# Bank order of projection bursts and scores, and a longer lag of the softmax normalization, in a layernorm + attention + gated FFN kernel

## The chip, the cores and the metric

The kernel runs on one core of a Trainium2 chip. The metric is the device time of one execution in microseconds. A core has a matmul engine (TensorE, PE in the profile; PEld is its weight load), three engines for elementwise work (VectorE = DVE, ScalarE = ACT, GpSimd = POOL) and a queue engine (SyncE = SP). The program gives each engine one list of instructions. TensorE's results go to PSUM, here used as eight banks of 512 fp32 columns over 128 partitions; in this kernel DVE and ACT read them from there, and POOL works on SBUF alone.

## The reference

```python
x = A_x                                   # (1, 2048, 448) bf16
xn = _layernorm(x)
# A: attention of 16 query heads on 8 key/value heads (Dh 256), last W = 512 keys of the cache, no mask
q = (xn @ wq) per head
p = softmax(q @ k.T * 256 ** -0.5)
s = concat(p @ v) @ wo
# B: gated FFN, F = 1792
g = silu((gelu(xn @ w_gate) * (xn @ w_up)) @ w_down)
return x + s * g
```

## The kernel before, in words

**Order of work.** The kernel records operations by hand with a small recorder: every call of `pe`, `act`, `dve`, `pool`, `dma` or `dmaT` appends one operation to one engine's list and derives its waits from the tiles and banks that it reads and writes. The order in the code is therefore the order on each engine, and what waits there holds up what was recorded behind it.

**Stages.** The 2048 rows are four chunks of 512 (four tiles of 128 rows each). First comes the FFN for all chunks (to about 133 us); the last chunk's `down` is spread as filler into the first attention heads. Then attention runs over `NI` = 64 pairs of chunk and head (`i` = 16 * chunk + head) with four tiles each, so `n = 4 * i + t` counts 256 tiles.

**One tile of attention.** `scores(i, t)` issues two matmuls into one PSUM bank, chosen by `s_bank(n)`; DVE takes the row maximum (L563, `nmax`), ACT the exponential with the row sum (L565, `pr` and `den`; the sum comes out with a second small instruction). `normalize` takes the reciprocal of the sum on DVE (L570) and scales `pr` (L575 on DVE; for the first 28 tiles L572 on POOL), and then issues a transposing DMA on SP's queue (L253) from `pr` to `pT`. `LAG` says how many tiles `normalize` stands behind `scores` in the recorded order: one. There are 11 `pr` buffers.

**What follows a tile.** At even `t`, `values` (four matmuls into bank 0, 6 or 1, by a fixed pattern of eight) multiplies the transposed probabilities of a head some three heads back with V; its result is copied to `oT`, by ACT (L599), in the first heads partly by DVE (L597). At odd `t`, from head 7 on, half an output projection `outproj` (L620) of a group of four heads is issued, mostly into bank 7, and DVE adds it to `acc` (L641, L643). In chunks after the first, head 6 of the chunk has no output projection and head 2 has two (the second one in place of values). The last head of each chunk is "folded": V times wo is made once, and its `pT` (`pTf`) goes straight into the output projection.

**Bursts.** The queries of the next eight heads are projected in one go: `q_burst` is called at tile `t = 0` of heads 7, 15, 23, ... 55, right behind that tile's scores and values (and a burst of four heads at i = 3). A burst has `heads` parts; part `n` fills a pair of banks, the matmuls (L473) coming in two phases, with phase 0 of part n+1 ahead of phase 1 of part n:

```python
for n in range(heads + 1):
    if n < heads:
        part(n, 0)
    if n:
        part(n - 1, 1)
```

Phase 0 has 8 half-height matmuls (two run side by side), phase 1 has 6. After phase 1 ACT copies both banks to `qT` (L528). Pair 0 is banks 0 and 1, pair 1 is 2 and 3, pair 2 is 4 and 5; banks 6 and 7 take no part. The banks of scores (2 to 5) and of values (0, 1) are thus used by bursts as well. I call the work between two bursts a stretch: 32 tiles.

**The end.** After the last scores (n = 255) one `normalize` is left, then two letters per step say what comes: "v" is a `values` of heads 61 and 62, "o" one of the three output projections left of the group of heads 56 to 59. Then come the output projections of the last group, the final DVE steps (L631, L633) and the output DMAs.

Of the kernel before, what the change touches and what calls it, by code (L numbers as in the profile page):

```python
# [144 lines left out]
def bass_recurrent_scan__sliding_block_cached__geglu_ffn__prompt_kernel(nc, A_x, A_k, A_v, A_wq, A_wo, B_x, B_wg, B_wu, B_wd, out):  # L145
# [6 lines left out]
    QC, TPC, HP, KF = 512, 4, 64, 3  # L152
# [9 lines left out]
    with es:  # L162
# [89 lines left out]
        def dmaT(dst, src, w=(), r=(), after=(), lane=None):  # L252
            return R.op("sync", lambda e: e.dma_start_transpose(dst, src), r=r, w=w, dma=True, after=after, lane=lane)  # L253
# [211 lines left out]
        def two_blocks(ph, c, s, w, w6, keys, q0=0, q1=QC):  # L465


            def run(e):
                for k in range(KF + 1 - ph):
                    for lo in (0, HP):  # L470
                        m = (lo > 0) ^ ph
                        lhsT = w[m][lo:lo + HP, k, :] if k < KF else w6[lo:lo + HP, :]
                        ins = e.matmul(bank(s + m)[:, q0:q1], lhsT=lhsT, rhs=xnT[lo:lo + HP, c, k, q0:q1],  # L473
                                       start=ph == 0 and k == 0, stop=ph == 1 and k == KF - 1)
                return ins
            hard = [phase0[s]] if ph else []
            phase0[s] = pe(run, r=xn(c)[q0 // P:q1 // P] + keys, w=[("ps", s), ("ps", s + 1)], hard=hard)
# [16 lines left out]
        def down(c, t, part=range(NF)):  # L494
            b = (6, 7, 3, 7)[t] if c == NQC - 1 else 6 + t % 2
            for f in part:
                pe(lambda e, f=f: e.matmul(bank(b, D), lhsT=actT[:, f, t * P:(t + 1) * P], rhs=wd[:, f, :],  # L497
                                           start=f == 0, stop=f == NF - 1),
                   r=[("actT", f), ("wd",)], w=[("ps", b)])
            if NF - 1 in part and c < NQC - 1:  # L500
                act(lambda e: e.activation(gy[:, c * TPC + t, :], bank(b, D), ACT.Copy),
                    r=[("ps", b)], w=[("gy", c * TPC + t)])
            elif NF - 1 in part:
                dve(lambda e: e.tensor_copy(gy[:, c * TPC + t, :], bank(b, D)),
                    r=[("ps", b)], w=[("gy", c * TPC + t)])


        NI = NQC * Hq
        NG = NI // 4

        def q_slot(i):

            p = i // 2
            p = p if p < 3 else (p - 3) % NQP
            return qT[p], "qT%d" % p, i % 2

        def q_burst(i0, heads):

            c, h0 = divmod(i0, Hq)

            def part(n, ph):
                hp, e_ = divmod(n, 2)
                s, h = 2 * ((2, 0, 1, 2, 0, 2, 1, 0)[n] if heads == 8 else (0, 1, 2, 0)[n] if i0 else (n + 2) % 4), h0 + 2 * hp
                buf, name, _ = q_slot(i0 + 2 * hp)
                two_blocks(ph, c, s, [wq[:, :, h + m, e_ * P:(e_ + 1) * P] for m in range(2)],
                           wq6[:, h // 2, e_ * P:(e_ + 1) * P], wq_keys)
                if ph:
                    act(lambda e: e.activation(  # L528
                        buf[:, :, e_, :], psum[:, s * 512:(s + 2) * 512].rearrange("p (a q) -> p a q", a=2), ACT.Copy, scale=scale),
                        r=[("ps", s), ("ps", s + 1)], w=[(name, e_)])  # L530
# [6 lines that stand above are left out]
# [4 lines left out]
        def p_slot(i):  # L541

            n = (i - i // Hq) % NPT
            return (pTf, ("pT", "f")) if folded(i) else (pT[:, n, :, :], ("pT", n))


        LAG, FIRST = 1, 7 * TPC

        def s_bank(n):
            return (4, 5, 2)[n % 3] if n <= 3 * TPC else 2 + (n + 1) % 4  # L550

        def scores(i, t):
            g, n = (i % Hq) // 2, i * TPC + t
            b, s = s_bank(n), n % NPR
            buf, name, a = q_slot(i)

            def run(e):
                for k in range(NE):
                    ins = e.matmul(bank(b), lhsT=buf[:, a, k, t * P:(t + 1) * P], rhs=kT[:, g, k, :],  # L559
                                   start=k == 0, stop=k == NE - 1)  # L560
                return ins
            pe(run, r=[("kT", g), (name, 0), (name, 1)], w=[("ps", b)])
            dve(lambda e: e.tensor_reduce(nmax[:, s:s + 1], bank(b), mybir.AxisListType.X, ALU.max, negate=True),  # L563
                r=[("ps", b)], w=[("nmax", s)])
            act(lambda e: e.activation(pr[s][:, :], bank(b), ACT.Exp, bias=nmax[:, s:s + 1], accum_out=den[:, s:s + 1]),  # L565
                r=[("ps", b), ("nmax", s)], w=[("pr%d" % s,), ("den", s)])

        def normalize(i, t):
            s = (i * TPC + t) % NPR
            dve(lambda e: e.reciprocal(rden[:, s:s + 1], den[:, s:s + 1]), r=[("den", s)], w=[("rden", s)])  # L570
            if i * TPC + t < FIRST:
                pool(lambda e: e.tensor_tensor(pr[s][:, :], pr[s][:, :], rden[:, s:s + 1].to_broadcast([P, W]), ALU.mult),  # L572
                     r=[("pr%d" % s,), ("rden", s)], w=[("pr%d" % s,)])
            else:
                dve(lambda e: e.tensor_scalar(pr[s][:, :], pr[s][:, :], rden[:, s:s + 1], None, op0=ALU.mult),  # L575
                    r=[("pr%d" % s,), ("rden", s)], w=[("pr%d" % s,)])
            dst, key = p_slot(i)
            dmaT(dst[:, :, t * P:(t + 1) * P], pr[s][:, :], r=[("pr%d" % s,)], w=[(*key, t)], lane="p%d" % s)
# [22 lines left out]
        def n_pieces(G):  # L601
            return 3 * NE + NJ if folded(4 * G + 3) else 4 * NE
# [55 lines left out]
        def silu(n):  # L658

            s = n % 2  # L660
            act(lambda e: e.activation(tmp[:, s, :], gy[:, n, :], ACT.Tanh, scale=0.5), r=[("gy", n)], w=[("tmp", s)])  # L661
            pool(lambda e: e.tensor_scalar(tmp[:, s, :], tmp[:, s, :], 1.0, 0.5, op0=ALU.add, op1=ALU.mult),  # L662
                 r=[("tmp", s)], w=[("tmp", s)])
            pool(lambda e: e.tensor_tensor(gy[:, n, :], tmp[:, s, :], gy[:, n, :], ALU.mult),
                 r=[("tmp", s), ("gy", n)], w=[("gy", n)])
# [35 lines left out]
        for i in range(NI):  # L701
            for t in range(TPC):
                n = i * TPC + t
                scores(i, t)
                if n >= LAG:
                    normalize(*divmod(n - LAG, TPC))
                if 4 * i + t in fill:
                    down(NQC - 1, *fill[4 * i + t])

                early = i >= Hq and i % Hq == 2  # L710
                if t % 2 == 0 and early:
                    n = n_pieces(outs[1][0])
                    outproj(*outs[1], range(n * t // 4, n * (t + 2) // 4), b=6)
                elif t % 2 == 0 and 4 * i + t >= 12:
                    values(*pv.pop(0))
                if 7 <= i and t % 2 and not (i >= Hq and i % Hq == 6):
                    n = n_pieces(outs[0][0])
                    outproj(*outs[0], range(n * (t - 1) // 4, n * (t + 1) // 4))
                    if t == TPC - 1:
                        del outs[0:1 + early]  # L720
                if t == 0 and (i == 3 or i % 8 == 7) and i + 1 < NI:
                    q_burst(i + 1, 4 if i == 3 else 8)
            if i % Hq in (7, 9, 11, 13):
                silu(i // Hq * TPC + (i % Hq - 7) // 2)
        for n in range(NI * TPC - LAG, NI * TPC):
            normalize(*divmod(n, TPC))

        for what in "vvovovo":
            if what == "v":
                values(*pv.pop(0))  # L730
            else:
                outproj(*outs[0], range(n_pieces(outs.pop(0)[0])))
# [35 lines left out]
```

## Time and profile before

| | us |
|---|---|
| median of 3 runs | 572.48 (572.27 to 572.71) |
| profiled execution, its own time | 572.64 |
| span of the profiled execution | 570.8 |
| PE busy | 556.0 (97%) |
| DVE busy | 369.5 (65%) |
| ACT busy | 369.6 (65%) |
| POOL busy | 117.1 (21%) |
| PE in the chain that ended last | 82% |
| granted clock of TensorE | 1.000 |

Times in the trace are counted from the start of the span. A row of the timeline gives start, duration, engine, line, operation, tile written and read, and in brackets the idle time of the engine just before it and what ended that. A row of the chain gives start, duration and what the end of the program was waiting for in that time. A row of waits gives who waited for whom: total us, times, longest. An SPq row covers the issuing of DMAs by SP. A busy share is an average over the span; a matmul's duration is modelled and overlaps the next one's.

### The profile page before, as it was taken

How to read it: one execution, taken by the hardware profiler on the slowest of the kernel's cores; microseconds unless marked ns; L12 is line 12 of the kernel's file. 1: busy time of each engine (PE TensorE's matmuls, PEld its weight loads, DVE VectorE, ACT ScalarE, POOL GpSimd, SP SyncE). 2: the span in 40 equal slices, each digit the busy share in tenths (PEclk: the TensorE clock that was granted, in tenths of full speed). 3: DMA queues.
4: the chain of work that ended last, by engine and by line, in shares of the span. 5: the costliest groups of instructions: out<-in, count | busy, mean ns of one | idle time of the engine just before them, and what ended most of it. 6: DMA issues, size and time to landing. Idle time of an engine off the chain costs nothing.

```text
span 570.8 us, 10398 instructions
## 1 busy us (share of the span) xinstructions
PE 556.0 (97%) x3550; PEld 261.9 (46%) x3550; DVE 369.5 (65%) x939; ACT 369.6 (65%) x800; POOL 117.1 (21%) x153
## 2 busy tenths in 40 slices
PE   9999999999999999999999999999999999999997
PEld 6444444444443444344444444444444344444445
DVE  5626345145481998199639936992898199739984
ACT  5433334247676687676778867776888676768860
POOL 0131223104481121003301110140121003301133
DMA  8882546922443455155625632545456155635552
GB/s 227 290 152 57 138 77 116 275 65 69 78 92 56 76 101 93 29 101 95 140 54 93 103 74 50 98 96 120 66 101 100 31 101 91 144 50 93 97 101 53
DMA packets 165445, 57.69 MB, mean 101 GB/s; under 512 B 155649, under 2 KB 162305, under 8 KB 165393
## 3 DMA queue, kind: packets, MB, share of 16 engines
q1 hardware_dynamic: 162048, 44.64, 41.5%
q0 software_dynamic: 3040, 12.16, 8.1%
q8 instruction: 29, 0.48, 0.4%
q10 hardware_dynamic: 304, 0.22, 0.2%
q14 instruction: 24, 0.19, 0.1%
HBM read 17.92 MB, written 1.84 MB: 35 GB/s over the span
## 4 chain that ended last, share of the span: by engine, by line
PE 82%; DVE 13%; ACT 2%; issue 1%; DMA 1%; POOL 0%; ACTq 0%
PE ps L473 32%; PE ps L559 15%; PE ps L590 15%; PE ps L620 12%; PE ps L497 7%; DVE nmax L563 7%; DVE pr L575 3%; ACT qT L528 1%; DVE acc L641 1%; DVE acc L643 1%; DVE rden L570 1%; PE ps L348 1%; ACT oT L599 1%; DMA pT<-pr 1%; DVE oT L597 0%
## 5 line engine op out<-in xcount | busy, mean ns | idle before, releaser
L563 DVE TENSOR_REDUCE nmax<-ps 128x1 f32<-128x512 f32 x256 | 175.0, 684 | 111.1 <-PE ps L559 107.7
L565 ACT ACTIVATE pr<-ps,nmax 128x512 bf16<-128x512 f32 x256 | 175.9, 687 | 69.7 <-PE ps L590 35.4
L559 PE MATMUL ps<-kT,qT 128*128 128x512 bf16 x512 | 150.9, 379 | 0.5 <-ACT qT L528 0.5
L590 PE MATMUL ps<-pT,V 128*128 128x512 bf16 x480 | 123.1, 379 | 2.1 <-ACT oT L599 1.4
L620 PE MATMUL ps<-wo,oT 128*128 128x448 bf16 (+1 forms) x498 | 111.0, 346 | 0.4 <-DVE acc L641 0.4
L473 PE MATMUL ps<-xnT,wq 64*128 64x512 bf16 x896 | 99.5, 376 | 7.9 <-ACT qT L528 7.8
L575 DVE TENSOR_SCALAR pr<-pr,rden 128x512 bf16<-128x512 bf16 x228 | 86.7, 380 | 8.1
L528 ACT ACTIVATE qT<-ps 128x1024 bf16<-128x1024 f32 x64 | 64.5, 1023 | 36.0 <-PE ps L473 35.3
L473 PE MATMUL ps<-xnT,wu 64*128 64x512 bf16 x336 | 82.3, 376 | 0.0
L473 PE MATMUL ps<-xnT,wg 64*128 64x512 bf16 x336 | 82.0, 376 | 0.0
L491 DVE TENSOR_TENSOR actT<-ps,hb 128x512 bf16<-128x512 f32 x56 | 38.5, 692 | 65.9 <-ACT hb L490 61.7
L559 PEld LDWEIGHTS ps<-kT,qT 128*128 128x128 bf16 x512 | 49.4, 98 | 55.8 <-issue 3.4
L590 PEld LDWEIGHTS ps<-pT,V 128*128 128x128 bf16 x480 | 46.3, 98 | 60.7 <-ACT oT L599 5.6
L473 PEld LDWEIGHTS ps<-xnT,wq 64*128 64x128 bf16 x896 | 44.0, 94 | 62.8 <-ACT qT L528 11.3
L620 PEld LDWEIGHTS ps<-wo,oT 128*128 128x128 bf16 x498 | 48.4, 98 | 49.5 <-DVE acc L641 1.9
L599 ACT ACTIVATE oT<-ps 128x512 bf16<-128x512 f32 x113 | 66.4, 588 | 4.6 <-PE ps L590 4.5
L490 ACT ACTIVATE hb<-ps 128x512 bf16<-128x512 f32 x56 | 33.1, 594 | 38.5 <-PE ps L473 38.4
L565 ACT ACTIVATION_READ_ACCUMULATOR pr<-ps,nmax 128x1 f32 x256 | 50.4, 197 | 0.0
L647 POOL TENSOR_TENSOR tmp<-acc,gy 128x448 f32<-128x448 f32 x16 | 16.6, 1035 | 149.3 <-DVE acc L643 141.2
L497 PE MATMUL ps<-wd,actT 128*128 128x448 bf16 x224 | 46.5, 353 | 0.0
L662 POOL TENSOR_SCALAR tmp<-tmp 128x448 f32<-128x448 f32 x16 | 9.1, 566 | 164.3 <-ACT tmp L661 164.3
L473 PEld LDWEIGHTS ps<-xnT,wg 64*128 64x128 bf16 x336 | 31.3, 94 | 20.5 <-issue 1.1
(62 smaller groups left out, 350.8 us busy)
## 6 DMA issues: line engine op xcount, KB each, us to landing
pT<-pr SPq DMA_TRANSPOSE x240, 2.5
wq<-in_A_wq_dram POOLq DMA_DIRECT2D x14, 256.0 KB, 3.6
wo<-in_A_wo_dram POOLq DMA_DIRECT2D x3, 896.0 KB, 8.1
V<-in_A_v_cache_dram POOLq DMA_DIRECT2D x4, 448.0 KB, 6.5
xr<-in_A_x_dram POOLq DMA_DIRECT2D x4, 448.0 KB, 4.6
wd<-in_B_w_down_dram SPq DMA_DIRECT2D x1, 1568.0 KB, 14.2
x<-in_A_x_dram SPq DMA_DIRECT2D x3, 448.0 KB, 8.3
out_dram<-xr POOLq DMA_DIRECT2D x3, 448.0 KB, 3.8
```

The lines of the kernel that those rows point to most:

```text
L473: ins = e.matmul(bank(s + m)[:, q0:q1], lhsT=lhsT, rhs=xnT[lo:lo + HP, c, k, q0:q1], start=ph == 0 and k == 0, stop=ph == 1 and k == KF - 1)
L490: act(lambda e: e.activation(hb[:, h, :], bank(s), ACT.Gelu_apprx_tanh), r=[("ps", s)], w=[("hb", h)])
L491: dve(lambda e: e.tensor_tensor(actT[:, f, :], bank(s + 1), hb[:, h, :], ALU.mult), r=[("ps", s + 1), ("hb", h)], w=[("actT", f)])
L497: pe(lambda e, f=f: e.matmul(bank(b, D), lhsT=actT[:, f, t * P:(t + 1) * P], rhs=wd[:, f, :], start=f == 0, stop=f == NF - 1), r=[("actT", ...
L528: act(lambda e: e.activation(buf[:, :, e_, :], psum[:, s * 512:(s + 2) * 512].rearrange("p (a q) -> p a q", a=2), ACT.Copy, scale=scale), ...
L559: ins = e.matmul(bank(b), lhsT=buf[:, a, k, t * P:(t + 1) * P], rhs=kT[:, g, k, :], start=k == 0, stop=k == NE - 1)
L563: dve(lambda e: e.tensor_reduce(nmax[:, s:s + 1], bank(b), mybir.AxisListType.X, ALU.max, negate=True), r=[("ps", b)], w=[("nmax", s)])
L565: act(lambda e: e.activation(pr[s][:, :], bank(b), ACT.Exp, bias=nmax[:, s:s + 1], accum_out=den[:, s:s + 1]), r=[("ps", b), ("nmax", s)], ...
L575: dve(lambda e: e.tensor_scalar(pr[s][:, :], pr[s][:, :], rden[:, s:s + 1], None, op0=ALU.mult), r=[("pr%d" % s,), ("rden", s)], w=[("pr%d ...
L590: ins = e.matmul(bank(b), lhsT=V[:, j, g, e_ * P:(e_ + 1) * P], rhs=src[:, j, :], start=j == 0, stop=j == NJ - 1)
L599: act(lambda e: e.activation(dst, bank(b), ACT.Copy), r=[("ps", b)], w=[key])
L620: ins = e.matmul(bank(b, D)[:, lo:hi], lhsT=lhsT, rhs=rhs, start=idx == 0, stop=idx == n8 - 1)
```

## The change

- The parts of every burst but the first take bank pairs 0, 1, 2, 0, 1, 2, ... in turn (before: 2, 0, 1, 2, 0, 2, 1, 0 for eight heads, 0, 1, 2, 0 for the four heads at i = 3, where nothing differs). The first burst keeps its order.
- `s_bank` is rewritten: tiles 13 to 28 go to banks 2, 3, 4, 5 in turn; from tile 29 on the order 4, 5, 2, 3 starts anew every 32 tiles, and the last tile of the 32 goes to bank 4.
- `LAG` is two. At n = `LAST` = 251 (last tile of head 62) tiles 249, 250 and 251 are all normalized right behind the scores of 251; nothing is normalized at 252, and tiles 252 to 254 then one tile behind.
- The order at the end is "vvoovvo" instead of "vvovovo".

```diff
-                s, h = 2 * ((2, 0, 1, 2, 0, 2, 1, 0)[n] if heads == 8 else (0, 1, 2, 0)[n] if i0 else (n + 2) % 4), h0 + 2 * hp
+                s, h = 2 * (n % 3 if i0 else (n + 2) % 4), h0 + 2 * hp
...
-        LAG, FIRST = 1, 7 * TPC
+        LAG, FIRST, LAST = 2, 7 * TPC, NI * TPC - TPC - 1
 
         def s_bank(n):
-            return (4, 5, 2)[n % 3] if n <= 3 * TPC else 2 + (n + 1) % 4
+            if n <= 3 * TPC:
+                return (4, 5, 2)[n % 3]
+            if n <= 7 * TPC:
+                return (2, 3, 4, 5)[(n - 3 * TPC - 1) % 4]
+            j = (n - 7 * TPC - 1) % (8 * TPC)
+            return (4, 5, 2, 3)[j % 4] if j < 8 * TPC - 1 else 4
...
                 scores(i, t)
-                if n >= LAG:
-                    normalize(*divmod(n - LAG, TPC))
+                for m in ((n - LAG,) if n < LAST else range(n - LAG, n + 1) if n == LAST else (n - 1,) if n > LAST + 1 else ()):
+                    if m >= 0:
+                        normalize(*divmod(m, TPC))
...
-        for n in range(NI * TPC - LAG, NI * TPC):
-            normalize(*divmod(n, TPC))
-
-        for what in "vvovovo":
+        normalize(NI - 1, TPC - 1)
+
+        for what in "vvoovvo":
```

## The prediction

> **What bounds the kernel now.** I read the page first (busy shares, then the chain that ended last), then the waits, the chain in order of time around bursts, and the timeline by engine at two places: ahead of a burst, and at the end.
>
> ```profile
> PE 556.0 (97%) x3550; PEld 261.9 (46%) x3550; DVE 369.5 (65%) x939; ACT 369.6 (65%) x800; POOL 117.1 (21%) x153
> PE 82%; DVE 13%; ACT 2%; issue 1%; DMA 1%; POOL 0%; ACTq 0%
> PE ps L473 <- ACT qT L528: 7.8, 7, 1.1
> ```
>
> TensorE (PE) is the bound: 97% busy and 82% of the chain. So an edit pays if PE stands still less. A matmul's shown time is longer than the spacing of a steady stream, so an idle figure understates a stall; I go by starts. The chain's row "42.09 21.26 PE ps L473 x196" is 98 pairs of half-height matmuls: 0.217 us a pair. The seven waits of L473 for the qT copy are one in each 8-head burst:
>
> ```profile
> 279.69 7.08 PE L473 MATMUL ps<-xnT,wq 64*128 64x512 bf16 x64
> 287.89 5.36 PE L473 MATMUL ps<-xnT,wq 64*128 64x512 bf16 x48 [1.11 <-ACT qT L528]
> 293.17 0.61 PE L559 MATMUL ps<-kT,qT 128*128 128x512 bf16 x2
> ```
>
> 32 pairs from 279.69 end the stream at 286.63; the next pair starts at 287.89. The stall is 1.26 us (1.28 start to start, the same in all seven). It is part 5, which takes pair 2 two parts after part 3 did. PE's other stalls in the attention stage, again by starts: 0.54 behind the 4-head burst at 154.45, four of 0.14 to 0.75 between 195 and 208 (1.66), six of 0.21 to 0.44 in mid-stretch (2.0), one of 0.21 at 549.36, and 0.66 for a transpose at 555.33. All stalls together are some 14 us; the rest of the span is matmuls.
>
> **The change, part by part.**
>
> *Bursts.* With part n on pair n % 3, each pair is reused three parts later. Phase 0 is 4 pairs (0.87), phase 1 is 3 (0.65). From the end of phase 1 of part n to phase 0 of part n+3 lie phase 0 of n+2 and phase 1 of n+1: 1.52 us. The copy takes 1.02, plus about 0.2 to its start and 0.06 from its end to PE: 1.28, so 0.24 to spare. Before's order already had this distance at parts 3, 4 and 7, and no gap shows in the 64-matmul run. All of 7 x 1.27 = 8.9 us goes. DVE idles through a burst, and ACT's 1.02 per 1.52 fits.
>
> *What the new first pair waits for.* A burst now begins on banks 0 and 1; the values two tiles earlier wrote bank 1, so its oT copy must be over. Before began on banks 4 and 5. Ahead of the bursts at 279.69, 386.88 and 494.07 (i = 23, 39, 55) head i-1 has no output projection, PE runs ahead, and ACT is late:
>
> ```profile
> 277.65 0.69 ACT L565 ACTIVATE pr<-ps,nmax 128x512 bf16<-128x512 f32 x1
> ...
> 278.76 0.69 ACT L565 ACTIVATE pr<-ps,nmax 128x512 bf16<-128x512 f32 x1 [0.33 <-PE ps L559]
> 279.35 0.19 ACT L565 ACTIVATION_READ_ACCUMULATOR pr<-ps,nmax 128x1 f32 x1
> 279.44 0.59 ACT L599 ACTIVATE oT<-ps 128x512 bf16<-128x512 f32 x1
> 279.92 0.69 ACT L565 ACTIVATE pr<-ps,nmax 128x512 bf16<-128x512 f32 x1
> ```
>
> The exps are of tiles 89, 90 and 91; the copy between is bank 1's. It ends at 280.03, so part 0 starts at 280.09 instead of 279.69: 0.40 lost, 1.2 over three bursts. Tile 92, now on bank 4 like tile 89, also waits: exp 89 ends at 278.34, and before's score 92 started at 278.22; 0.17 that lies inside the 0.40. Part 1 (bank 2, tile 91) needs 280.61 and is due at 280.96. At i = 15, 31, 47 the copy is done a full us before the burst, at i = 7 it is a DVE copy ending at 171.02, just when the burst began; DVE then stood four times 0.24 to 0.40 waiting for ACT's sum, which the longer lag removes. I take 0 for these four.
>
> *Banks behind the 4-head burst.* Tile 13 goes to bank 2, whose pair was copied at 152.88, instead of bank 4 (154.39). 0.54 won.
>
> *Normalization two tiles behind.* The count of DVE instructions is the same, so where DVE is saturated (the mid-stretch stalls) nothing moves: these 3.6 us stay and are what is late next. The reciprocal's waits on ACT (7 of them, 1.8 us) end, but only one (0.1 at 204.6) was ahead of a PE stall. What also shifts is every transpose: one tile later in SP's queue, which is nearly full:
>
> ```profile
> 539.44 13.81 SPq L253 DMA_TRANSPOSE pT<-pr  x10
> 553.35 5.17 SPq L253 DMA_TRANSPOSE pTf<-pr  x4
> 552.04 3.15 DMA pT<-pr
> ```
>
> 14 issues from 539.44 to 558.52 are 1.31 to 1.36 each; a stretch's tile takes 1.24. So SP falls behind within each stretch and recovers in the burst. A tile deferred over the burst comes first in the next stretch, and all behind it land 1.3 later relative to PE. The values that read them had these margins from landing to start: 1.28 us for head 4 (values at 170.06), 2.2 to 2.8 for the tightest of later stretches. So head 4 is at zero (cost 0 to 0.2), the others hold. I set this against the 0.1 above: 0.
>
> *The end.* At n = 251 three tiles are normalized between two reductions, tile 251 only after its own exp; and by the new function tiles 252 and 253 both lie on bank 4, with no burst between them. Before:
>
> ```profile
> 546.49 0.69 ACT L565 ACTIVATE pr<-ps,nmax 128x512 bf16<-128x512 f32 x1
> 547.06 0.21 ACT L565 ACTIVATION_READ_ACCUMULATOR pr<-ps,nmax 128x1 f32 x1
> 548.04 0.69 ACT L565 ACTIVATE pr<-ps,nmax 128x512 bf16<-128x512 f32 x1 [0.78 <-PE ps L590]
> 547.28 0.68 DVE L563 TENSOR_REDUCE nmax<-ps 128x1 f32<-128x512 f32 x1
> 547.53 0.59 PE L559 MATMUL ps<-kT,qT 128*128 128x512 bf16 x2
> ```
>
> Exp 251 ends its sum at 547.27. Then reciprocal 251 (0.19 to the next start), scaling (0.27), accumulation (0.53): reduction 252 starts at 548.29, 1.0 later than at 547.28. Exp 252 follows by 0.77 and ends at 549.75; score 253, in before at 547.53, starts at 549.81: PE stands 2.28 us, and behind it queue all its last scores, values and projections. Against that the 0.21 at 549.36 goes, and the 0.66 at 555.33: two projections (1.51 each instead of one) stand ahead of values(62, 0), due now at 558.2, while its transpose, one slot later, lands near 556. Normalizing head 62 at once gains nothing, since SP was 3.6 us behind (tile 251 scaled by 548.41, issued at 552.04). Net: 2.28 - 0.21 - 0.66 = 1.4 lost. If DVE reached tile 252 without delay, exp 252 would still end at 548.73 and cost 1.26, net 0.4: the lower bound. Upper: 2.5.
>
> A stall of 2.3 us is longer than any in the attention stage so far. The granted clock is 1.00 in every window of before, with seven stalls of 1.27; I add nothing for the clock here. [...] What it would do at 2.3 us is the third rival.
>
> **Sum,** in the profiled execution (572.64 us, span 570.8): 8.9 - 1.2 + 0.54 - 1.4 = 6.8 won, 565.8. The three runs' median is 572.48, 0.16 lower: 565.7.
>
> **Rivals.**
> *The end costs nothing* (tiles 252 and 253 do not collide, or DVE gets there early): the 0.87 of the two stalls is won instead of 1.4 lost, 563.4. For it: the tail's DVE has idle time from 550; against: the bank function gives 4 twice. Chance 0.12.
> *ACT or the transposes are later at bursts*: one more tile of ACT delay (1.1) at the three late bursts and a slow SP issue (up to 2.4 in the L253 rows, 1.1 over the usual) ahead of tight values give 3.3 back or a little more: 569. Chance 0.10.
> *The clock drops in the last stall.* In before's start 32 matmuls of 128 columns take 3.60 us, 0.112 each, where a quarter of 0.217 is 0.054: half speed for 3.6 us. Once more at the end this costs 1.8: 567.5. Chance 0.04.
> *Slower: the bubble is not removed but spread.* If a copy together with its two hops took 1.5 instead of 1.28 behind the late first pair, each of the parts 3 to 7 would wait about 0.2 and a burst would lose its 1.27 again; then 0.54 - 1.2 - 1.4 leaves 574.5. It decides from 1.0 us left per burst. Against it: the unbroken run through parts 3 and 4. Chance 0.04. This is also the case in which the change doesn't do what it says.
>
> **Numbers.** The forecast has 0.70. The range is 563.2 to 568.3: down to the first rival (563.4) less the 0.1 to 0.2 of the reciprocal's wait; up over the clock (567.5) to the end at its upper bound (1.1 more), one late burst with a tile more of delay (1.1) and head 4's 0.2, 568.1. It leaves out most of the second rival and the slower one. A measurement tells about 0.2%, 1.1 us, from no change: faster 0.94, same 0.01, slower 0.05.
>
> **What would show it.** Right: L473's wait for qT gone from the waits; bursts of 112 matmuls in some 12.2 us without a gap; part 0 of the three late bursts 0.4 behind the values; a PE stall of about 2.3 us before the second score of the last head, ended by ACT pr; no DMA in the chain at the end; mid-stretch stalls as before. Wrong: a qT wait in the burst, PE waiting for pT in mid-stretch, or no stall at score 253.

## The result, and the profile after

The changed kernel takes 566.98 us (median of 6 runs, 565.44 to 567.75); the kernel before took 572.60 beside it (6 runs, 571.87 to 573.15). The ratio is 0.9898, with a 95% interval of 0.9882 to 0.9914: faster by about 1%. The forecast was 565.7 (563.2 to 568.3), and faster.

The profiled execution of the changed kernel took 567.38 us, with a span of 565.6. The new lines of code shift the numbers: scores are L564, the row maximum L568, exp L570, reciprocal L575, scaling L580, values L595, copies to `oT` L604, output projections L625, accumulation L648. First the page: the engines, the granted clock in 40 slices, and the group of the bursts' matmuls, whose last column is the idle time ahead of them; under them one row of the waits.

```profile
PE 553.2 (98%) x3517; PEld 261.2 (46%) x3550; DVE 368.1 (65%) x939; ACT 369.7 (65%) x800; POOL 116.8 (21%) x153
PEclk9999999999999999999999999999999999999989
L473 PE MATMUL ps<-xnT,wq 64*128 64x512 bf16 x896 | 98.3, 376 | 0.4
PE ps L564 <- ACT pr L570: 2.2, 1, 2.2
```

TensorE no longer waits for a qT copy: in all 896 matmuls of the bursts 0.4 us of idle time is left. In its place stands one wait of 2.2 us, of a score for an exp. The PEclk row has something that before did not have: an 8 in the slice before the last. (Weight loads count 3550, matmuls 3517: 33 matmul records are missing, each of which looks like a gap of one matmul, 0.19 to 0.22 us, in the timeline. One such place also cuts this trace's chain short, so I don't use the chain.)

The timeline around the first of the three late bursts (i = 23), TensorE's rows and two of ACT's:

```profile
274.71 1.30 PE L564 MATMUL ps<-kT,qT 128*128 128x512 bf16 x4
...
277.01 12.26 PE L473 MATMUL ps<-xnT,wq 64*128 64x512 bf16 x112
...
274.57 0.69 ACT L570 ACTIVATE pr<-ps,nmax 128x512 bf16<-128x512 f32 x1
...
276.36 0.59 ACT L604 ACTIVATE oT<-ps 128x512 bf16<-128x512 f32 x1
```

All 112 matmuls now stand in one row. By starts, from the first of the burst to the score behind it, a burst takes 12.19 us where it took 13.49, 1.30 less. (The first score behind it is one of the missing records here, and its place is taken from the second. An expectation below has 12.10 and 13.40: these are counted to the end of the last pair, 0.1 short of the score in both kernels.) Ahead of it two short waits are new. The second of the two scores in the first row (tile 92, bank 4) waits 0.26 for exp 89, whose row is the first of ACT's and whose sum comes out at 275.35. And part 0 starts at 277.01, just behind the copy that ends at 276.95; that is 0.29 behind the steady stream, 0.1 of which the switch to half-height matmuls takes where nothing is waited for, too (0.09 at i = 15 and 31, whose bursts start at 224.26 and 329.26).

And the end, in rows of PE, DVE and ACT:

```profile
538.30 1.03 PE L595 MATMUL ps<-pT,V 128*128 128x512 bf16 x4
541.54 0.60 PE L564 MATMUL ps<-kT,qT 128*128 128x512 bf16 x2 [2.21 <-ACT pr L570]
541.98 1.29 PE L625 MATMUL ps<-wo,oT 128*128 128x448 bf16 x4
543.07 1.06 PE L564 MATMUL ps<-kT,qT 128*128 128x512 bf16 x2
...
538.94 0.16 DVE L575 RECIPROCAL rden<-den 128x1 f32<-128x1 f32 x1
539.14 0.35 DVE L580 TENSOR_SCALAR pr<-pr,rden 128x512 bf16<-128x512 bf16 x1
539.41 0.62 DVE L648 TENSOR_TENSOR acc<-ps,acc 128x448 f32<-128x448 f32 x1
539.94 0.68 DVE L568 TENSOR_REDUCE nmax<-ps 128x1 f32<-128x512 f32 x1
...
540.70 0.69 ACT L570 ACTIVATE pr<-ps,nmax 128x512 bf16<-128x512 f32 x1 [1.80 <-issue]
```

Tile 251's reciprocal, scaling and the accumulation hold reduction 252 until 539.94; exp 252 then ends its sum at 541.48, and score 253 on the same bank starts at 541.54. The four values before it start 0.216 apart, the last at 538.95, so TensorE stands from 539.17 to 541.54: 2.37 us. Behind it the four projection matmuls show 1.29 us and the two scores 1.06, where elsewhere such rows show 0.92 and 0.59. That is a lower clock. In half-microsecond windows (columns: length, busy time of PE, PEld, DVE, ACT and POOL, granted clock, DMA share, GB/s):

```profile
542.00:542.50 0.50, 0.50 (x4) 0.29 (x3) 0.32 (x1) 0.00 (x0) 0.00 (x0) 0.88 0.56 110
542.50:543.00 0.50, 0.50 (x3) 0.15 (x1) 0.47 (x3) 0.04 (x1) 0.00 (x0) 0.50 0.10 18
...
545.50:546.00 0.50, 0.40 (x2) 0.22 (x2) 0.00 (x0) 0.35 (x3) 0.00 (x0) 0.70 0.96 185
546.00:546.50 0.50, 0.50 (x3) 0.23 (x3) 0.15 (x1) 0.47 (x1) 0.00 (x0) 1.00 0.40 78
```

0.88 is a clock of 0.5 for 0.12 us, so half speed begins at 542.38; 0.70 ends it at 545.80. By an estimate from this, the 3.42 us at half speed cost half their length, 1.7 us: TensorE is busy for all 3.42 of them.

The ledger of the two profiled executions, by the starts of the bursts (us won; the span fell by 5.2):

| where | forecast | measured |
|---|---|---|
| seven 8-head bursts | +8.9 | +9.1 (13.49 to 12.19 each) |
| stretches ending in the three late bursts | -1.2 | -1.17 (0.39 each) |
| up to the burst at i = 7 | +0.54 | +0.37 (0.54, less 0.17 for head 4's pT) |
| from there to the burst at i = 15 | 0 | +0.26 |
| after the last burst | -1.4 | -3.18 (-2.37, -1.7 for the clock, +0.21, +0.66) |
| up to the first burst | 0 | -0.14 |
| sum | +6.8 | +5.24 |

### The profile page after: what moved, and what is told of

It is laid out like the page before. It is cut to its first block, busy times and chain, and to the rows that moved or that the text cites. A ratio compares the mean times of both kernels' runs of the same rounds, so it can differ in the third digit from the quotient of the medians.

```text
span 565.6 us, 10365 instructions
## 1 busy us (share of the span) xinstructions
PE 553.2 (98%) x3517; PEld 261.2 (46%) x3550; DVE 368.1 (65%) x939; ACT 369.7 (65%) x800; POOL 116.8 (21%) x153
## 5 line engine op out<-in xcount | busy, mean ns | idle before, releaser
L568 DVE TENSOR_REDUCE nmax<-ps 128x1 f32<-128x512 f32 x256 | 175.0, 684 | 109.4 <-PE ps L564 105.5
L570 ACT ACTIVATE pr<-ps,nmax 128x512 bf16<-128x512 f32 x256 | 175.9, 687 | 71.4 <-PE ps L595 32.5
L564 PE MATMUL ps<-kT,qT 128*128 128x512 bf16 x488 | 146.6, 380 | 4.7 <-ACT pr L570 2.2
L595 PE MATMUL ps<-pT,V 128*128 128x512 bf16 x471 | 122.5, 381 | 2.7 <-ACT oT L604 1.7
L625 PE MATMUL ps<-wo,oT 128*128 128x448 bf16 (+1 forms) x498 | 111.2, 347 | 0.4 <-DVE acc L646 0.4
L473 PE MATMUL ps<-xnT,wq 64*128 64x512 bf16 x896 | 98.3, 376 | 0.4
L580 DVE TENSOR_SCALAR pr<-pr,rden 128x512 bf16<-128x512 bf16 x228 | 86.6, 380 | 8.1
L564 PEld LDWEIGHTS ps<-kT,qT 128*128 128x128 bf16 x512 | 49.3, 98 | 59.3 <-issue 4.8
L595 PEld LDWEIGHTS ps<-pT,V 128*128 128x128 bf16 x480 | 46.6, 98 | 60.5 <-ACT oT L604 4.9
L625 PEld LDWEIGHTS ps<-wo,oT 128*128 128x128 bf16 x498 | 48.5, 98 | 49.2 <-DVE acc L646 1.6
L604 ACT ACTIVATE oT<-ps 128x512 bf16<-128x512 f32 x113 | 66.5, 588 | 4.0 <-PE ps L595 4.0
L570 ACT ACTIVATION_READ_ACCUMULATOR pr<-ps,nmax 128x1 f32 x256 | 50.3, 197 | 0.0
L473 PEld LDWEIGHTS ps<-xnT,wu 64*128 64x128 bf16 x336 | 31.3, 94 | 19.9
```

Of the source, the lines that this page charges most:

```text
L595: ins = e.matmul(bank(b), lhsT=V[:, j, g, e_ * P:(e_ + 1) * P], rhs=src[:, j, :], start=j == 0, stop=j == NJ - 1)
L604: act(lambda e: e.activation(dst, bank(b), ACT.Copy), r=[("ps", b)], w=[key])
L625: ins = e.matmul(bank(b, D)[:, lo:hi], lhsT=lhsT, rhs=rhs, start=idx == 0, stop=idx == n8 - 1)
```

## The experiments

Eleven kernels; the changed kernel is the base unless another is named. The end first, where the forecast and the profile differ.

**One bank at the end.** Tile 252 goes to bank 3, so that it no longer shares bank 4 with tile 253.

```diff
-            return (4, 5, 2, 3)[j % 4] if j < 8 * TPC - 1 else 4
+            return (4, 5, 2, 3)[j % 4] if j < 8 * TPC - 1 or n > LAST else 4
```

> The changed kernel with one bank moved: tile 252, the first of the last head, goes to bank 3 instead of bank 4, so that the scores of tiles 252 and 253 no longer share a bank. Theory (the stall before score 253 is the shared bank, made longer by the three normalizations ahead of reduction 252): score 253 starts without a wait; reduction 252 stays 1.0 us late, so the values at tile 254 wait about 1.1 us for the oT copy of bank 6; net 1.1 us won over the executions of the changed kernel whose clock stayed at 1.00 (566.0), so 564.9, and the clock stays at 1.00 in every execution, because no gap of over 1.3 us is left. Rival (reduction 252 alone is the cause, whatever the bank): a stall of about 2 us stays ahead of the last head's scores or values, time 566 to 567.4, and the clock still drops in some executions.

Measured: 564.50 (564.12 to 564.57), ratio 0.9857 [0.9841, 0.9874], granted clock 1.00 in all four executions. Score 253 waits no more; what is late next is a projection and a values:

```profile
539.63 0.93 PE L625 MATMUL ps<-wo,oT 128*128 128x448 bf16 x4 [0.32 <-DVE acc L648]
...
541.58 1.04 PE L595 MATMUL ps<-pT,V 128*128 128x512 bf16 x4 [0.58 <-ACT oT L604]
```

By starts these are 0.48 (which was not expected) and 0.75 (1.1 was) in place of 2.37: the shared bank and not DVE's order alone makes the long gap. The two that are left come to 1.23 together, about half of it, with matmuls between, and the clock stays at 1.00.

**The same, and no normalization at once.** On top of the last kernel, the lag of two is kept to the end.

```diff
-                for m in ((n - LAG,) if n < LAST else range(n - LAG, n + 1) if n == LAST else (n - 1,) if n > LAST + 1 else ()):
+                for m in (n - LAG,):
...
-        normalize(NI - 1, TPC - 1)
+        for n in range(NI * TPC - LAG, NI * TPC):
+            normalize(*divmod(n, TPC))
```

> As the run before, and head 62 is not normalized at once: the lag of two tiles goes on to the end, and the last two tiles are normalized behind the loop. Theory (SP's queue was 3.6 us behind there, so normalizing at once brings no transpose forward and only delays reduction 252): reduction 252 is back at its time, the stall at the values of tile 254 shrinks to about 0.2, values of head 62 still find their transpose landed because two projections stand ahead of them; 0.9 us less than the run before, 564.0. Rival (normalizing at once is needed by the values of head 62): PE waits for a pT transpose near the end, by 0.5 us or more, and the time is not below the run before.

Measured: 563.79 (562.99 to 564.53), ratio 0.9844 [0.9827, 0.9862]. The two stalls go, and 0.21 comes back at 541.24; but the values of head 62 now wait 0.58 for their transpose, which they did not in the kernel with the three at once:

```profile
548.63 1.67 PE L595 MATMUL ps<-pT,V 128*128 128x512 bf16 x7 [0.41 <-DMA pT<-pr]
```

So normalizing head 62 at once does bring that transpose forward. It costs 1.23 of stalls (0.48 and 0.75) and saves 0.79 (0.21 and 0.58). This balance of 0.44 is read from the rows: the times of the two kernels overlap (564.12 to 564.57 and 562.99 to 564.53) and don't show it.

**Lag of one everywhere.** `LAG = 1`, the loop as in the last diff, the shared bank 4 kept.

> The changed kernel with the normalization one tile behind everywhere, as before the change, and so without the three at n = 251; tiles 252 and 253 still share bank 4. Theory (the lag of two tiles buys nothing and at the end the shared bank costs 1.26 us even when reduction 252 comes at its time): a gap of 1.26 us before score 253, no wait for pT at the end, clock 1.00 in every execution; bursts, the burst at i = 3 and the late bursts as in the changed kernel: 572.6 - 9.1 - 0.5 + 1.2 + 0.4 = 564.6, and up to 0.5 more where the burst at i = 7 waits for a DVE copy behind ACT's sums. Rival (the lag of two is part of the win): 566 or more, with new waits of PE for DVE or ACT in mid-stretch.

Measured: 565.13 (564.29 to 565.41), ratio 0.9865 [0.9851, 0.9878]; clock 1.00 in all four. The gap before score 253 is 1.35 (expected 1.26). With the shared bank kept and the three normalizations gone, a stall of the predicted lower bound is left. This kernel is 1.85 faster than the changed kernel, and 0.9 faster than those of its executions that kept their clock (566.02 on average): the lag of two with its exception at tile 251 is the part of the change that did not pay. A lag of one together with tile 252 on bank 3 was not run.

**A shorter gap.** Tile 251 is normalized behind scores 252, not at once.

```diff
-                for m in ((n - LAG,) if n < LAST else range(n - LAG, n + 1) if n == LAST else (n - 1,) if n > LAST + 1 else ()):
+                for m in ((n - LAG,) if n < LAST else range(n - LAG, n) if n == LAST else (n - 1,)):
```

> The changed kernel with tile 251 normalized behind scores 252 instead of 251, so that reduction 252 waits for two normalizations and for no exp; the gap before score 253 shrinks to about 1.7 us. Theory (length of the gap decides): the clock stays at 1.00 in all or nearly all executions, and the time is 566.0 - 0.6 = 565.4. Rival (any gap above the 1.3 us of before can do it): below 1.00 in about half of them again.

Measured: 565.20 (564.98 to 566.05), ratio 0.9871 [0.9858, 0.9885]. The gap is 1.81 and the clock 1.00 in all four.

**A longer gap.** Two reductions whose result nobody uses stand ahead of reduction 252.

```diff
+                if n == LAST:
+                    for x in (14, 15):
+                        dve(lambda e, x=x: e.tensor_reduce(nmax[:, x:x + 1], bank(s_bank(LAST)), mybir.AxisListType.X, ALU.max, negate=True),
+                            r=[("ps", s_bank(LAST))], w=[("nmax", x)])
```

> The changed kernel with two reductions more on DVE (0.6 us each, their results unused) between the three normalizations and reduction 252, so that PE's gap before score 253 grows from 2.37 to 3.57 us. Theory (the longer the gap, the surer it lowers the granted clock, and matmuls behind it then run at half speed for some 4 us): the clock is below 1.00 in all executions instead of half of them; 566.0 + 1.2 + 1.5 = 568.7. Rival (the clock dropped in half of the executions for a reason that has nothing to do with the gap): still about half of them, two groups at 567.2 and 568.7.

Measured: 568.07 (566.46 to 568.76), ratio 0.9914 [0.9899, 0.9928]. The gap is 3.56 as expected, but the clock was lower (0.997) in three executions of five only. The profiled one is among the other two: behind its gap the scores show 0.60 and the projection 0.92, full speed.

```profile
542.32 0.60 PE L564 MATMUL ps<-kT,qT 128*128 128x512 bf16 x2 [3.40 <-ACT pr L570]
542.76 0.92 PE L625 MATMUL ps<-wo,oT 128*128 128x448 bf16 x4
```

That speaks against "all executions": the length of the gap alone does not decide.

**A much longer gap.** The same with eight such reductions (and `nmax` widened to hold their results).

> The changed kernel with eight unused reductions ahead of reduction 252 in place of none: TensorE's gap before score 253 grows from 2.37 to about 7.1 us, 4.75 more. Theory: the chance that the clock falls grows with the gap's length and is 1 at this length; granted clock 0.997 or lower in every execution, half speed for some 4 us behind the gap, 567.5 + 4.75 = 572.2 in all. Rival: length beyond 2.4 us does not matter, the clock falls in about half of the executions as with gaps of 2.4 and 3.6 us, and the times split into some near 570.8 and some near 572.2.

Measured: 572.12 (571.35 to 572.79, 11 runs), ratio 0.9992 [0.9983, 1.0000]. The gap is 7.15, and the clock is below 1 in all 11 executions: 0.994 in nine, 0.991 in two. In one-microsecond windows of the profiled one (columns as above):

```profile
541.00:542.00 1.00, 0.00 (x0) 0.00 (x0) 1.00 (x3) 0.00 (x0) 0.00 (x0) 0.96 0.44 97
542.00:543.00 1.00, 0.00 (x0) 0.00 (x0) 1.00 (x3) 0.00 (x0) 0.00 (x0) 0.50 0.58 131
...
548.00:549.00 1.00, 1.00 (x5) 0.40 (x3) 0.07 (x1) 0.47 (x2) 0.00 (x0) 0.63 0.00 0
```

Half speed runs from 541.92 to 548.74 by the same arithmetic: 6.82 us, twice the 3.42 above. The theory held, but for the slow time, which it put at some 4 us.

**The turn alone.** The kernel before, with only the banks of the bursts' parts changed.

```diff
-                s, h = 2 * ((2, 0, 1, 2, 0, 2, 1, 0)[n] if heads == 8 else (0, 1, 2, 0)[n] if i0 else (n + 2) % 4), h0 + 2 * hp
+                s, h = 2 * (n % 3 if i0 else (n + 2) % 4), h0 + 2 * hp
```

> The kernel before with the bursts' pairs taken in turn and nothing else. Theory (the bubble goes, but the score banks of before do not fit the new order): the seven waits inside bursts go (9.1 us, 1.30 each as the changed kernel's bursts of 12.10 against 13.40 show), but part 1 now needs banks 2 and 3, which hold the last two tiles: it waits 1.2 us at the burst of i = 7, 0.3 at i = 15, 31, 47 and, with part 0's 0.4, 1.07 at i = 23, 39, 55, together 5.3 back; 572.6 - 9.1 + 5.3 = 568.8. Rival (first parts wait for nothing that matters): 563.5.

Measured: 570.33 (569.71 to 570.95), ratio 0.9958 [0.9943, 0.9972]. The direction holds, the size is 1.5 short. At i = 23:

```profile
279.25 1.04 PE L473 MATMUL ps<-xnT,wq 64*128 64x512 bf16 x8 [0.41 <-ACT oT L599]
280.97 11.40 PE L473 MATMUL ps<-xnT,wq 64*128 64x512 bf16 x104 [0.68 <-ACT pr L565]
```

Parts 0 and 1 wait 0.57 and 0.84 (by starts) at the three late bursts, part 1 alone 0.47 at i = 15, 31 and 47 (0.3 was expected), and 0.25 and 1.16 at i = 7. The transpose at the end is waited for 1.04 us instead of 0.66. So some 6.4 of the bursts' 9 us are lost again where the scores' banks do not fit the turn. With the new `s_bank` part 1 waits nowhere, at a lag of one neither.

**The lag alone.** The kernel before with `LAG = 2`.

> The kernel before with the lag of the normalization at two tiles and nothing else. Theory (no DVE work is saved, mid-stretch stalls stay, and all transposes of a stretch come one slot of 1.3 us later): the wait for pT at the end grows from 0.66 us to 1.4 to 1.9, everything else stays; 573.3 to 573.8. Rival (the lag frees DVE from waiting for ACT's sums and shortens the mid-stretch stalls of 3.6 us): 571 or less.

Measured: 573.34 (572.77 to 574.28, 11 runs), ratio 1.0012 [1.0003, 1.0021]. Where before waited 0.66, it now waits 1.34:

```profile
556.41 1.02 PE L590 MATMUL ps<-pT,V 128*128 128x512 bf16 x4 [1.18 <-DMA pT<-pr]
```

In SP's queue the transpose that it waits for is issued at 553.69 instead of 552.04: one slot of 1.31, and 0.34 by which the whole queue is later there. Of the slot 0.68 reaches the wait: the values start 2.72 behind that issue (556.41), in before 3.29 (555.33). Head 4's values wait 0.18 (at 170.74), the stalls behind i = 7 fall from 1.66 to 1.41, and those in mid-stretch stay as they were.

**What is late next in mid-stretch.** The second kernel above (563.79), with the tiles still pending normalized right behind each burst's issue.

```diff
+        done = 0
...
-                for m in (n - LAG,):
-                    if m >= 0:
-                        normalize(*divmod(m, TPC))
+                while done <= n - LAG:
+                    normalize(*divmod(done, TPC))
+                    done += 1
...
                     q_burst(i + 1, 4 if i == 3 else 8)
+                    while done <= i * TPC + t:
+                        normalize(*divmod(done, TPC))
+                        done += 1
```

> The version of e2_tail_lag2 (tile 252 on bank 3, lag of two to the end) with one thing more: at each burst the tiles still unnormalized are normalized right behind it, while DVE has nothing to do. Theory (mid-stretch stalls come from DVE being saturated between bursts, and the wait for pT from SP's queue, so work moved into the burst shortens both): DVE has 0.9 us less to do in each stretch, the six mid-stretch stalls of 0.21 to 0.44 and the 0.21 near the end go (2.2 us), 0.4 of those behind the burst of i = 7, and the 0.58 of wait for pT: 563.8 - 3.2 = 560.6. Rival (the stalls are set by the banks of values, not by DVE's load): they stay, only the wait for pT goes, 563.2.

Measured: 563.18 (563.01 to 563.54), ratio 0.9833 [0.9819, 0.9846]. The waits for transposes go, but the six mid-stretch stalls (three of 0.44, three of 0.21) stay, each ahead of a values and ended by an `oT` copy. The theory that DVE's load behind a burst makes them falls.

**The banks of values.** On top of it, the fixed pattern of eight is replaced by one of sixteen in which no two consecutive values in mid-stretch lie on bank 6 (and the last one before the tail goes to bank 1).

```diff
-            b = (0, 6, 0, 6, 0, 1, 6, 6)[at % 8] if at < 2 * NI else (0, 6, 1, 0, 6, 1)[at - 2 * NI]
+            b = (0, 6, 0, 6, 0, 1, 6, 0, 1, 6, 0, 6, 0, 1, 6, 6 if at < 2 * NI - 1 else 1)[at % 16] if at < 2 * NI else (0, 6, 1, 0, 6, 1)[at - 2 * NI]
```

> The kernel with tiles still pending normalized behind each burst (563.18 us), with only the banks of values changed: no two consecutive values lie on bank 6 in mid-stretch or before the last head's end. Theory: the six stalls of 0.44 and 0.21 in mid-stretch and the one of 0.21 at the end come from the second of two values on bank 6 waiting for the copy of the first; all seven go, 3 x 0.44 + 4 x 0.21 = 2.2 won, 561.0. Rival: they come from DVE's or ACT's load, which a bank only makes visible; then the stalls reappear at the next score or at the three late bursts, and the time stays at 562.5 to 563.2.

Measured: 561.06 (560.87 to 561.19), ratio 0.9797 [0.9784, 0.9811]. The timeline's row of one of the values, first without this edit, then the same values with it:

```profile
258.77 1.04 PE L595 MATMUL ps<-pT,V 128*128 128x512 bf16 x4 [0.28 <-ACT oT L604]
```

```profile
257.43 1.03 PE L595 MATMUL ps<-pT,V 128*128 128x512 bf16 x4
```

All seven stalls are gone, and an eighth of 0.68 at 205.94, which I had not counted: 2.85 in all. At the end 0.66 of waiting for pT appears, by my reading because TensorE comes there earlier and SP doesn't; 2.2 remain, and 2.1 were measured. (That the sum met the expected 561.0 so well is these two errors cancelling.)

**The late bursts.** On top of that, the values two steps ahead of the three late bursts go to bank 7.

```diff
-            b = (... 0, 6, 0, 1, 6, 6 if at < 2 * NI - 1 else 1)[at % 16] ...
+            b = (... 0, 6, 0, 7 if at % 32 == 13 and at > 32 else 1, 6, 6 if at < 2 * NI - 1 else 1)[at % 16] ...
```

> The same as e9_value_banks, and the values two tiles ahead of the bursts behind i = 23, 39 and 55 go to bank 7 (free there) in place of bank 1, so that part 0 does not need their copy. Theory: part 0 waits only for that bank; 3 x 0.2 less than e9_value_banks (561.0), 560.4, and the wait of 0.26 before tile 92's scores (exp 89 on the same bank) stays. Rival: ACT is behind at this place whatever the bank, and part 1 or the bank of tile 91 takes the wait over: no difference from e9_value_banks.

Measured: 560.75 (560.43 to 561.21), ratio 0.9792 [0.9779, 0.9806]. Part 0 no longer waits, but a late burst now takes 12.28 us instead of 12.19, so about half of the 0.2 is lost inside it, as the rival has it. The 0.3 between the medians is less than the runs of each spread; I call the two kernels equal. They are the best of the study, 2.0 and 2.1% under before, and the last is about 1.1% under the changed kernel (0.9792 / 0.9898 = 0.989).

## Why the prediction was right, and where it was not

*Bursts.* Right: 1.30 each instead of 1.27, no gap left. The rival that spreads the bubble is excluded by the single row of 112 matmuls.

*The first pair.* Right in place and size: 0.39 against 0.40 per late burst, nothing at i = 15, 31 and 47. The split differed. I put the wait of tile 92's scores inside part 0's; both show, one after the other (0.26, and 0.2 beyond the usual switch). The turn alone shows what this step also rests on: with the old banks of scores, part 1 waits as well. I worked the waits of that kernel out some 0.2 too small at each of the six later bursts; why is open.

*The 4-head burst and the lag.* 0.54 came, and head 4's values took 0.17 of it (0 to 0.2 was given). That DVE no longer waits for ACT's sums gave 0.26 (0.1 was given). The lag by itself costs 0.6 by the rows: 0.68 at the end, from the one slot in SP's queue that was foreseen, and 0.18 at head 4, less 0.25 behind i = 7. In the changed kernel the exception at 251 hides that slot, at a price that is higher than what it hides.

*Mid-stretch stalls.* Right that they stay, wrong on why. I laid them to a saturated DVE because DVE was busy there. The release named in the row was an ACT copy of a values' bank, and the pattern (0, 6, 0, 6, 0, 1, 6, 6) puts two values in a row on bank 6. Taking the load off around the burst left them, changing the bank removed them.

*The end.* The gap was 2.37 against 2.28, by the chain that was worked out: reciprocal, scaling, accumulation, reduction, exp, shared bank. That normalizing head 62 at once gains nothing was wrong by the 0.58 that its absence costs.

*The clock.* This is the term that was mis-sized: 0 in the sum, 1.7 in the profile, and with it the end costs 3.18 instead of 1.4. The rival had the mechanism, with a chance of 0.04; it came in three of six executions. Those three average 567.49 and the three others 566.02, which is 0.3 from the forecast; the median of 566.98 lies between the two groups, where no execution is. My reason was that no stall up to 1.3 us had lowered the clock; the step from there to 2.3 had no row under it. That the rival's price (1.8) came out so well was luck: its 3.6 us were the length of the first row of matmuls in before, and the slow start outlasts that row (four matmuls of L348 still take 0.63 from 5.37 on, eight take 0.62 from 6.99 on; the granted clock of the windows shows 1.00 all the same).

*Why only some executions.* No run shows it. With the gap of 2.37 the clock was lower in three of six executions, with 3.56 in three of five, with 7.15 in 11 of 11, with 1.81 and 1.35 in none of four each. So the longest gap always lowered it and the two shortest never did; between them the length alone does not decide, as the traced gap of 3.56 kept its clock and the traced one of 2.37 did not. When the half speed began differs as well: 0.84 us behind the end of the gap of 2.37 (541.54 to 542.38), and 3.22 us into the one of 7.15 (538.70 to 541.92). Executions without a trace show only their mean clock: 0.997, 0.994 and 0.991 are 1.7, 3.4 and 5.1 us short of full clock in 566 to 570, by an estimate 3.4, 6.8 and 10.2 us at half speed. The traces have 3.42 and 6.82; the third length is in none.

## What to carry to other kernels

When a bank, a buffer or an order is made to fit at one place, work out what shares it at the last place where the pattern runs (here two tiles of the last head on one bank): an exception that is right ahead of six bursts left the kernel's longest stall ahead of the end, where no burst follows. Read a stall by the release that its row names and the buffers of the two operations, not by which engine is busy around it; six stalls put down to DVE were a pattern of banks. A stall on TensorE may cost more than its length (here one of 2.37 us cost 1.7 on top in the traced execution, and the clock was lower in three of six), so shorten it before anything else at that place. Stalls of up to 1.81 left the clock at 1.00 here; that matmuls put into the middle of a stall would save the clock, with the idle time unchanged, was not run.

## What the hardware showed that was not expected

A gap of 2.37 us in TensorE's work lowered the granted clock in three of six executions (0.997 on average over the span). In the traced one it fell to half 0.84 us after TensorE had resumed, for 3.42 us, so the matmuls that run slowly are not those right behind the gap (two scores and two projection matmuls still ran at 0.22 and 0.19 us each). A gap one and a half times as long (3.56) was passed over in two executions of five, the traced one among them, and one of 7.15 us lowered the clock in all 11 executions, in the traced one at 541.92, while TensorE still stood (to 545.85), so that part of the slow time was spent idle: against the two executions with a gap of 3.56 at full clock (566.46 and 567.44, mean 566.95) its median is 5.2 us longer, 3.6 of them the longer gap itself. That leaves 1.6 for 6.82 us at half speed, since only the last 2.9 of these (from 545.85) had matmuls in them.
